# A chunked linear-attention layer and its squared-ReLU MLP on one core: first chunk loaded as pairs of tokens, second weight matrix on SyncE's queue

## The chip, the cores and the metric

The kernel runs on one core of a Trainium2 chip. A core has a matrix engine (TensorE, PE in the profile; its weight loads are PEld), a vector engine (VectorE, DVE), a scalar engine (ScalarE, ACT), GpSimd (POOL) and SyncE (SP), which here only issues transfers. SBUF is the on-chip memory with 128 partitions; PSUM holds what TensorE writes, in eight banks of 128 x 512 fp32. Sixteen DMA engines move data between HBM and SBUF. The metric is the device time of one execution in microseconds (us), the median of several runs.

## The reference

Two stages: an attention with a decaying state, then a feed-forward with squared ReLU. With B = 4 batches, H = 8 heads, S = 768 tokens, D = 48:

```python
for t in range(S):
    cur = np.einsum('bhd,bhe->bhde', u[None] * kt, vt)
    y[:, :, t] = np.einsum('bhd,bhde->bhe', rt, state + cur)
    state = w[None, :, :, None] * state + np.einsum('bhd,bhe->bhde', kt, vt)
x = y.transpose(0, 2, 1, 3).reshape(3072, 384)
h = np.maximum(x @ w_in, 0.0)          # w_in  384 x 2048
out = (h * h) @ w_out                  # w_out 2048 x 384
```

## The kernel before

The sequence is cut into six chunks of L = 128 tokens. A unit is one batch's chunk; unit i is batch i mod 4 of chunk i div 4, so there are 24, and units 0 to 3 are the first chunk, with no state yet. Inside a chunk the recurrence becomes products of matrices: r and k are scaled by powers of w (rows count up for r, down for k), a masked 128 x 128 product of them per head weighs v, the state of the chunk before adds its part, and the diagonal term with u is done elementwise.

The order of all work is written out by hand as a string, ORDER: 966 steps, each with a name, its indices, the engine (A ScalarE, D VectorE, G GpSimd, P TensorE, S SyncE) and the buffers it takes. Each engine gets its own steps in this order and works through them in order. The names:

- ld.x.i loads r, k or v of unit i: 128 tokens on 128 partitions, 8 pieces of 48 floats (192 bytes) for each. w and u load the decay and bonus rows; shw and shu spread them over the partitions (wb, ub); logw, Wk, Wt, WkS, WtS make the powers of w; wc, WLcol, WLm the power for a whole chunk.
- kh.i and rh.i multiply k and r by those powers into rk (bf16); T.i transposes rk on TensorE (eight transposes into one bank) and Tc.i copies it to rkT. From unit 7 on XB.i does this by a transposing transfer.
- A.i: eight products (four pairs of heads by two heads) of rkT into two banks; Bm.i.h masks them. Y.i: Bm by v (vb, bf16), plus rkT by the state S0W from chunk 1 on. U.i: k by v, for the state; S0, ts and S update it.
- P0, P1, du, dv: the diagonal term; xs.i adds it to Y. X.i and xTc.i (or the transfer xX.i) transpose x into xT.
- F1.g.s: x by W1 for group g of units, 512 columns of one bank; re and sq are ReLU and square. F2.i.q: four products of unit i with quarter q of W2, added up in one bank; os.i copies the sum, out.i stores it. F2c splits the last unit by columns.
- lW.0.s loads slice s of W1 in fp32 to a staging buffer wsa, cW.0.s casts it to bf16. W.0.2 (a slice of W1) and W.1.0 to W.1.3 (W2) are transfers on GpSimd's queue that cast on the way.
- Z.n.b is filler: n products of identity by identity (in fours, as one product of 512 columns) into bank b.

GROUPS lists how many units share one F1: units 0 and 1 are groups of one (products of 128 columns), all others pairs (256 columns). PSUM is split: four banks for attention ("bank"), two for F1 ("bH"), two for F2 ("bO"); the powers of w for the first chunk live in the last two ("early").

Of the kernel before, what the change touches and what calls it, by code (L numbers as in the profile page):

```python
# [28 lines left out]
Y.2:P/1 xs.2:D/2 re.1.3:A/0 X.0:P/3 F1.1.0:P/0 xTc.0:A/1 F1.0.0:P/1 dv.3:G Y.3:P/2 xs.3:D/3 X.2:P/1 ld.r.4:S/4 U.0:P/3
re.1.0:A/1 xTc.2:A/0 W.1.0:G F1.0.3:P/0 cW.0.5:G W.1.1:G X.3:P/2 cW.0.4:A xTc.3:A sq.1.0:A0/0 re.0.0:D/2 ld.k.4:S/4  # L30
ld.r.5:S/5 U.3:P/1 F1.0.2:P/1 WLcol:A re.0.3:D/3 ld.k.5:S/5 re.0.2:D/4 F1.1.2:P/0 sq.0.0:A0/1 W.1.2:G W.1.3:G ld.k.7:S/6
re.1.2:D/5 F1.2.1:P/1 ld.v.5:S/4 WkS:A F1.2.4:P/0 cW.0.3:G re.2.1:A/1 F1.2.5:P/1 re.2.4:D/2 U.1:P/2 F1.2.7:P/0
sq.0.2:A0/2 re.2.5:A/4 sq.1.3:D2/3 re.2.7:A/0 sq.2.1:D2/4 sq.2.4:D2/5 F1.0.1:P/1 F1.1.1:P/0 sq.0.3:D2/6 re.0.1:A/1
F1.2.3:P/1 re.1.1:A/2 sq.1.1:A0/7 sq.1.2:D2/8 WLm:G F2.0.0:P/1 S0.0:D re.2.3:D/3 F1.2.2:P/0 F2.1.0:P/0 F1.2.6:P/1 S0.3:D
re.2.2:A/2 F1.2.0:P/0 P0.4:G/4 sq.0.1:D2/9 kh.7:G/4 ld.v.4:S/5 F2.1.1:P S0.1:D ld.r.7:S/6 rh.4:D/5 sq.2.7:A0/10 kh.4:D
sq.2.5:A0/11 F2.0.1:P T.4:P/3 S0.2:D sq.2.3:A0/12 P0.5:G/0 sq.2.2:A0/13 rh.5:D/6 F2.0.2:P P1.4:D re.2.0:A/5 Tc.4:A/4
kh.5:D F2.1.2:P ld.r.6:S/2 ld.k.6:S/0 sq.2.0:D1/14 P1.5:G A.4:P/1/2 T.5:P/0 Tc.5:A/5 du.4:D/4 F2.0.3:P Bm.4.0:D/2
ld.v.7:S/6 F2.1.3:P os.0:D/0 os.1:A/1 A.5:P/3/0 Bm.4.1:D/0 vb.4:A/4 vb.5:A/5 F2.3.0:P/1 re.2.6:A/1 F2.2.0:P/0 Bm.5.0:D/4
ld.r.9:S/0 F2.2.1:P Y.4:P/1 du.5:D/0 Bm.5.1:D/5 U.5:P/2 Y.5:P/3 vb.7:A/6 dv.4:G F2.2.2:P sq.2.6:D1/15 ld.k.9:S/1
xs.4:D/4 dv.5:G rh.7:G F2.3.1:P X.4:P/0 kh.6:G/3 xs.5:D/0 X.5:P/1 ld.v.6:S/0 ts.5:D/0 P0.7:D/1 xTc.5:A/1 rh.6:D F2.3.2:P  # L40
xTc.4:A P1.7:D XB.7:S/6 F2.2.3:P kh.9:D/2 P0.9:D/3 T.6:P/3 rh.9:D F1.3.4:P/0 ld.k.10:S/2 F2.3.3:P Tc.6:A/0 P0.6:D/2
ld.k.8:S/3 vb.6:A/7 re.3.4:A/0 F1.3.3:P/1 A.6:P/2/1 re.3.3:A/4 ld.r.8:S/1 P1.6:G ld.v.8:S/1 os.3:D/2 A.7:P/0/3
F1.3.1:P/0 du.7:D/1 F1.3.5:P/1 S.5:G Bm.6.0:D/3 kh.8:G/1 U.7:P/2 Bm.6.1:D/1 ld.v.10:S/2 re.3.1:A/3 du.6:D/2 re.3.5:A/2
dv.6:G Bm.7.1:D/2 U.4:P/1 Bm.7.0:D/0 sq.3.3:A0/16 F1.3.0:P/0 F1.3.2:P/1 re.3.0:A/5 sq.3.1:A0/17 Y.6:P/3 dv.7:G Y.7:P/0
ld.v.9:S/3 F1.3.7:P/0 ts.4:D/1 XB.9:S/1 out.3:S re.3.2:A/1 xs.6:D/1 sq.3.0:A0/18 vb.8:A/2 U.6:P/1 os.2:D/3 rh.8:G
kh.10:G/0 X.6:P/3 XB.8:S/3 sq.3.2:A0/19 ld.k.11:S/4 F1.3.6:P/1 F2.5.0:P/1 ld.r.10:S/3 F2.4.0:P/0 xs.7:D/2 X.7:P/0
F2.4.1:P xTc.6:A/2 ld.r.11:S/4 F2.5.1:P ts.7:D/0 re.3.6:A/4 re.3.7:D/3 xTc.7:A F1.4.4:P/1 P0.8:G/4 kh.11:G/6 F1.4.6:P/0
S.4:D ld.r.12:S/5 ld.k.13:S/5 sq.3.7:A0/20 ts.6:D/1 P1.8:D sq.3.4:A0/21 du.8:D/3 ld.r.13:S/6 sq.3.5:A0/22 S.7:D
# [69 lines left out]
def kernel(  # L118
# [66 lines left out]
    def bank(var, kind="b"):  # L185
        return banks[first[kind] + slot[var]]
# [65 lines left out]
    def loaded(x, i):  # L252
        return ld[x][slot[f"{x}{i}"]]
# [308 lines left out]
```

## Time and profile before

| | us |
|---|---|
| median of 3 runs | 174.04 (173.41 to 174.83) |
| profiled execution, span | 172.5 |
| TensorE busy | 161.6 |
| VectorE busy | 130.3 |
| ScalarE busy | 111.1 |
| GpSimd busy | 80.8 |
| of TensorE: F1 products (line 445) | 74.9 |
| F2 products (line 472) | 69.3 |
| filler (line 498) | 9.5 |

Times in the profile count from the first instruction of the span. A busy matrix engine is not one at its peak: products are pipelined, and a product's listed duration is its passage, not its distance to the next. In rows of the timeline the columns are start, duration (of the first to the last of a run of equal instructions), engine, line, operation, what is written and read, count, and in brackets the idle time before and what ended it. In rows of the groups come the count, the busy time and the mean in ns, then the idle time before them. In rows of the windows come, for each engine, busy time and instructions, then the granted clock, the busy share of the DMA engines and GB/s.

### The profile page before, as it was taken

The numbers are of one execution on the slowest core, as the hardware profiler recorded it, in microseconds if no ns is written. First come the engines' busy times: TensorE is split into PE (matmuls) and PEld (weight loads), VectorE is DVE, ScalarE is ACT, GpSimd is POOL, SyncE is SP. The second block draws the span as 40 slices with busy tenths as digits, with TensorE's granted clock in tenths as the row PEclk, the third lists the DMA queues.
The fourth block names the chain that finished last, engine by engine and source line by source line (L and its number), as shares of the span: only waits on it lengthen the run. The fifth ranks groups of instructions, "written<-read, shape, count | busy, mean of one in ns | idle before, by whom it ended". The sixth has DMA issues, their size and how long they took to land.

```text
span 172.5 us, 4388 instructions
## 1 busy us (share of the span) xinstructions
PE 161.6 (94%) x1702; PEld 121.2 (70%) x1702; DVE 130.3 (76%) x259; ACT 111.1 (64%) x207; POOL 80.8 (47%) x98
## 2 busy tenths in 40 slices
PE   3976799979999999999999999999999999999992
PEld 1444788745788787787778768777778778777671
DVE  5768977739999896598789889888889894538300
ACT  2358787746379899858649647848858726532430
POOL 5644895108659298966937364047660204000000
PEclk9999999999999999999999999999999999999999
DMA  5999899989999989979999997998988330331022
GB/s 99 223 244 306 227 188 207 195 166 200 204 212 184 202 177 214 241 174 184 204 189 215 177 229 153 180 181 186 154 217 159 85 114 4 87 141 48 23 78 84
DMA packets 105588, 29.13 MB, mean 169 GB/s; under 512 B 98008, under 2 KB 105568, under 8 KB 105568
## 3 DMA queue, kind: packets, MB, share of 16 engines
q1 hardware_dynamic: 103672, 26.95, 72.7%
q0 software_dynamic: 1744, 1.77, 6.1%
q8 instruction: 13, 0.21, 0.5%
q10 hardware_dynamic: 152, 0.14, 0.2%
q14 instruction: 7, 0.06, 0.1%
HBM read 20.46 MB, written 4.72 MB: 146 GB/s over the span
## 4 chain that ended last, share of the span: by engine, by line
PE 76%; DMA 12%; SPq 8%; ACT 1%; POOL 1%; issue 1%; DVE 0%; POOLq 0%
PE bank L472 33%; PE bank L445 31%; DMA ldk<-in_k_dram 8%; SPq L320 6%; DMA wsa<-in_moe_w_in_dram 4%; PE bank L376 3%; PE bank L394 2%; PE bank L392 2%; SPq L324 2%; PE bank L403 2%; PE bank L486 2%; PE bank L429 1%; PE bank L363 1%; ACT W L260 1%; POOL urow L218 0%
## 5 line engine op out<-in xcount | busy, mean ns | idle before, releaser
L445 PE MATMUL bank<-xT,W 128*128 128x256 bf16 (+1 forms) x624 | 74.9, 264 | 0.2
L472 PE MATMUL bank<-W,hq 128*128 128x384 bf16 x368 | 69.3, 326 | 0.0
L453 ACT ACTIVATE hr<-bank 128x512 bf16<-128x512 f32 x75 | 44.4, 596 | 32.6 <-PE bank L445 27.1
L445 PEld LDWEIGHTS <-W 128*128 128x128 bf16 x624 | 55.2, 98 | 10.6 <-DVE hr L455 0.3
L472 PEld LDWEIGHTS <-hq 128*128 128x128 bf16 x368 | 34.8, 98 | 17.6
L460 ACT ACTIVATE hq<-hr 128x512 bf16<-128x512 bf16 x65 | 39.1, 628 | 0.3
L384 DVE TENSOR_TENSOR Bm<-bank,maskJT 128x512 bf16<-128x512 f32 x48 | 31.3, 684 | 7.3 <-PE bank L376 7.2
L346 POOL TENSOR_TENSOR P<-P,ub 128x384 f32<-128x384 f32 x15 | 16.1, 1079 | 13.9 <-DVE P L342 13.6
L455 DVE TENSOR_SCALAR hr<-bank 128x512 bf16<-128x512 f32 x21 | 14.3, 687 | 8.5 <-ACT hq L460 3.8
L342 POOL TENSOR_TENSOR P<-ldr,ldk 128x384 f32<-128x384 f32 x14 | 14.3, 1022 | 9.6 <-DMA ldk<-in_k_dram 6.0
L336 POOL TENSOR_TENSOR rk<-ldk,Wkhat 128x384 bf16<-128x384 f32 x10 | 10.0, 996 | 16.9 <-DMA ldk<-in_k_dram 16.9
L411 DVE TENSOR_TENSOR xs<-bank,dv 128x384 bf16<-128x384 f32 x24 | 13.0, 552 | 5.0 <-POOL dv L354 2.8
L354 POOL TENSOR_TENSOR dv<-ldv,du 128x384 f32<-128x384 f32 x18 | 14.8, 829 | 0.0
L349 DVE TENSOR_REDUCE du<-P 128x8 f32<-128x384 f32 x24 | 13.0, 544 | 0.6 <-POOL P L346 0.4
L260 ACT COPY rkT<-bank 128x1024 bf16<-128x1024 bf16 x7 | 7.1, 1012 | 9.1 <-PE bank L363 9.1
L339 POOL TENSOR_TENSOR rk<-ldr,Wt 128x384 bf16<-128x384 f32 x9 | 9.0, 996 | 7.0 <-DMA ldr<-in_r_dram 7.0
L260 ACT CAST vb<-ldv 128x384 bf16<-128x384 f32 x19 | 9.6, 511 | 4.1 <-DMA ldv<-in_v_dram 4.1
L498 PE MATMUL bank<-identity 128*128 128x512 bf16 x29 | 9.5, 471 | 2.7 <-POOL identity masks.py:199 2.7
L260 ACT COPY os<-bank 128x384 f32<-128x384 f32 (+1 forms) x15 | 7.0, 469 | 6.8 <-PE bank L472 4.5
L262 DVE COPY os<-bank 128x384 f32<-128x384 f32 (+1 forms) x10 | 5.2, 524 | 7.9 <-PE bank L486 4.3
L394 PE MATMUL bank<-vb,Bm 128*128 128x48 bf16 x192 | 11.0, 183 | 0.0
L464 DVE TENSOR_TENSOR hq<-hr 128x512 bf16<-128x512 bf16 x27 | 10.9, 432 | 0.0
(66 smaller groups left out, 166.5 us busy)
## 6 DMA issues: line engine op xcount, KB each, us to landing
ldk<-in_k_dram SPq DMA_DIRECT2D x24, 192.0 KB, 3.6
ldr<-in_r_dram SPq DMA_DIRECT2D x24, 192.0 KB, 3.6
ldv<-in_v_dram SPq DMA_DIRECT2D x24, 192.0 KB, 4.0
out_dram<-os SPq DMA_DIRECT2D x23, 192.0 KB, 2.3
wsa<-in_moe_w_in_dram SPq DMA_DIRECT2D x7, 384.0 KB, 5.6
W<-in_moe_w_out_dram POOLq DMA_DIRECT2D x4, 384.0 KB, 9.9
rkT<-rk SPq DMA_TRANSPOSE x17, 3.5
W<-in_moe_w_in_dram POOLq DMA_DIRECT2D x1, 192.0 KB, 6.3
```

The lines of the kernel that those rows point to most:

```text
L260: e.copy(o, a)
L342: e.tensor_mul(P0b[slot[f"P{i}"]], loaded("r", i), loaded("k", i))
L346: e.tensor_mul(t, t, ub)
L349: e.tensor_reduce(dub[slot[f"dv{i}"]], P0b[slot[f"P{i}"]], axis=mybir.AxisListType.X, op=ALU.add)
L354: e.tensor_mul(dvb[slot[f"dv{i}"]], loaded("v", i), t)
L384: e.tensor_mul(Bmb[slot[f"Bm{i}{h}"]], heads(bank(f"bA{i}{h}"), 128), mask_b)
L394: e.matmul(y[:, hc, D * h : D * (h + 1)], m[h][:, hc, :], vb[:, 2 * hc + h, :], start=(c == 0), stop=True, skip_group_check=True,)
L445: e.matmul(hp[:, fi, :], W1[f // 2][:, c, 128 * (f % 2) : 128 * (f % 2 + 1)], xt[:, c, :], start=(c == 0), stop=(c == CCH - 1), skip_group ...
L453: e.activation(hr, hp, AF.Relu)
L455: e.tensor_scalar_max(hr, hp, 0.0)
L460: e.activation(hq, hr, AF.Square)
L472: e.matmul(bank(f"bO{i}", "bO")[:, 0:d_model], hqb[slot[f"hq{g},{f // m}"]][:, at : at + L], W2[q][:, f % 4, :], start=(f == 0), stop=(f = ...
```

## The change

- **The first chunk in pairs.** Batches 0 and 1, and batches 2 and 3, are loaded together: batch 2p to partitions 0 to 63 and batch 2p + 1 to partitions 64 to 127, two neighbouring tokens on one partition. A piece is then 384 bytes; there are 12 such transfers (ldp) in place of 12 ld. Unit 2p + j now means the tokens of parity j of both batches. Two sets of powers of w are made (Wkp, Wtp), one for each parity, from column exponents that GpSimd writes.
- **Products on quarters.** Rows 0 to 63 and 64 to 127 belong to different batches, so A of units 0 to 3 is done for each half of rows apart (16 products, 64 output partitions each), Y sums over both parities (32 products of 64 rows, 64 output partitions and 48 columns), and U runs once for a pair (16 products of 64 rows) and gives both batches' state. T and Tc of these units are done apart for r and k, four transposes into half a bank.
- **W2 by SyncE.** The DMA casts on GpSimd's queue are gone. W2 comes in eight slices in fp32 (lW.1.s), each partition reading two whole rows (3,072 bytes) and W1 in eight (lW.0.s), through nine shared staging buffers st (also those of the pairs); cW casts them, on ScalarE six times, GpSimd nine times, VectorE once.
- **w** is spread by one transfer to all 128 partitions on SyncE's queue, without wrow and shw.
- **GROUPS** is twelve pairs; the eight PSUM banks are one pool; F2 may take W2's parts in any order (F2.i.f0.nf starts at product f0), and `summed` tells which product is the first and the last of a bank.
- **ORDER** is new throughout (976 steps).

The start of the new order:

```
tab:A nat:G ldp.r.0.1:S/0 w:S logw:A Wtp.0:A ldp.r.0.0:S/0 rh.0:D/0 Z.60.7:P T.r.0:P/0 Wtp.1:A rh.1:D/0 T.r.1:P/0
ldp.k.0.1:S/1 Wkp.1:A ldp.k.0.0:S/1 kh.1:G/1 Wkp.0:A kh.0:D/1 Tc.r.1:A/0 u:S shu:D ldp.k.1.0:S/2 Tc.r.0:A/0 Z.10.7:P
T.k.1:P/1 Tc.k.1:A/1 Z.16.7:P A.1:P/2/3 P0.1:D/0 P0.0:G/1 P1.1:D du.1:D/0 ldp.k.1.1:S/2 kh.2:D/2 T.k.0:P/1 kh.3:G/2
ldp.r.1.0:S/3 T.k.3:P/4 ldp.r.1.1:S/3 rh.2:G/3 P0.3:D/2 wc:S Bm.1.1:D/0 WkS:A Tc.k.0:A/1 Z.8.0:P A.0:P/5/6 Bm.0.1:D/1
Bm.0.0:D/2 Bm.1.0:D/3 T.r.2:P/7 rh.3:G/3 Z.7.0:P T.r.3:P/7 P1.0:G ldp.v.0.1:S/4 ldp.v.0.0:S/4 dv.1:G vb.1:A/0 du.0:D/1
T.k.2:P/4 dv.0:D vb.0:A/1 U.p0:P/0/1 Z.13.6:P Y.0:P/3 ld.r.4:S/0 xs.0:D/0 Tc.r.2:A/2 Y.1:P/6 xs.1:D/1 Tc.r.3:A/2 Tc.k.2:A/3
A.2:P/5/7 Bm.2.1:D/4 P1.3:G du.3:D/2 WtS:A ld.k.4:S/0 WLcol:A WLm:G S0.0:D lW.0.5:S/5 cW.0.5:G Tc.k.3:A/3 kh.4:G/4 lW.0.2:S/6
cW.0.2:A A.3:P/2/4 Bm.3.0:D/5 X.0:P/3 xTc.0:A/0 ldp.v.1.0:S/7 X.1:P/6 xTc.1:A/0 ld.k.5:S/1 kh.5:D/5 ldp.v.1.1:S/7 vb.2:A/2
rh.4:G/4 F1.0.2:P/7 re.0.2:A/0 F1.0.5:P/3 re.0.5:A/1 T.4:P/0 Bm.2.0:D/0 ld.r.5:S/1 rh.5:D/5 lW.0.6:S/8 cW.0.6:A vb.3:G/3
U.p1:P/6/2 P0.2:G/3 dv.3:G Bm.3.1:D/1 T.5:P/5 Tc.4:A/4 lW.0.1:S/0 cW.0.1:G P1.2:D Y.2:P/7 F1.0.6:P/3 re.0.6:A/2 S0.2:D
...
```

Its last three steps on TensorE are F2.22.4.4, F2c.23.0 (256 columns) and F2c.23.1 (128 columns); before, the last unit, 22, had its 128 columns first and its 256 columns last.

The core of the rest:

```diff
-GROUPS = [1, 1, 2, 2, 2, 2, 2, 2, 2, 2, 2, 2, 2]
+GROUPS = [2, 2, 2, 2, 2, 2, 2, 2, 2, 2, 2, 2]
+    stb = bufs("st", [128, CCH * 256], FP32)
...
+    def two(x, b):
+        t = src[x]
+        return bass.AP(
+            tensor=t.tensor, offset=t.offset + b * H * S * D,
+            ap=[[2 * D, L // 2], [S * D, H], [1, 2 * D]],
+        )
...
+        def ldp(e, x, p, b):
+            e.dma_start(out=staged(f"{x}P{p}").rearrange("p (h x) -> p h x", h=H)[rows[b]], in_=two(x, 2 * p + b))
...
         def lW(e, a, s):
+            t = staged(f"ws{a}{s}")
+            if a == 0:
+                e.dma_start(out=t.rearrange("p (c n) -> p c n", c=CCH), in_=w_in_t[:, :, 256 * s : 256 * (s + 1)])
+            else:
+                e.dma_start(out=t, in_=w_out_p[s])
...
-        def W(e, a, s):
-            e.dma_start(out=rows2(W2[s], s) if a else W1[s], in_=weights(a, s))
...
         def A(e, i):
+            if i < B:
+                tk, tr = [rkTb[slot[f"rkT{x}P{i // 2}"]].rearrange("q (j c) t -> q j c t", j=2) for x in "kr"]
+                for hc in range(HP):
+                    for h in range(2):
+                        q = slice(64 * h, 64 * h + D)
+                        for p in rows:
+                            e.matmul(
+                                heads(bank(f"bA{i}{h}"), 128)[p, hc, :].rearrange("p (j t) -> p j t", j=2),
+                                tk[q, i % 2, hc, p],
+                                tr[q, :, hc, p],
+                                start=True, stop=True, skip_group_check=True,
+                            )
+                return
...
         def Y(e, i):
+            if i < B:
+                both = [i - i % 2, i - i % 2 + 1]
+                at = slice(64 * (i % 2), 64 * (i % 2) + 64)
+                for hc in range(HP):
+                    for h in range(2):
+                        for z in both:
+                            for p in rows:
+                                e.matmul(
+                                    y[p, hc, D * h : D * (h + 1)],
+                                    Bmb[slot[f"Bm{z}{h}"]][p, hc, at],
+                                    vbb[slot[f"vb{z}"]][p, 2 * hc + h, :],
+                                    start=(z == both[0]), stop=(z == both[1]), skip_group_check=True,
+                                )
+                return
...
         def U(e, i):
+            if isinstance(i, str):
+                n = int(i[1:])
+                for hc in range(HP):
+                    for j in range(2):
+                        for b, p in enumerate(rows):
+                            e.matmul(
+                                heads(bank(f"bU{2 * n + b}"), 2 * D)[:, hc, :],
+                                pair(rk[slot[f"rkkP{n}"]][p], j, hc),
+                                vbb[slot[f"vb{2 * n + j}"]][p, 2 * hc : 2 * hc + 2, :].rearrange("p a b -> p (a b)"),
+                                start=(j == 0), stop=(j == 1), skip_group_check=True,
+                            )
+                return
...
-        def F2(e, i, q):
+        def F2(e, i, f0, nf):
...
-            for f in range(4 * q, 4 * q + 4):
+            for f in range(f0, f0 + nf):
                 at = L * n * (f % m) + L * j
+                summed[i] += 1
...
-                    start=(f == 0), stop=(f == FCH - 1), skip_group_check=True,
+                    start=(summed[i] == 1), stop=(summed[i] == FCH), skip_group_check=True,
```

More of the change, by code (lines that the diff above doesn't have):

```diff
@@ L32 @@
[L32 to L36, printed above, removed]
```

365 lines of the change are left out of this document (203 added, 162 removed).

## The prediction

> **What bounds the kernel now.** I read the page's head first, then the windows, the chain, and the timeline of the first 40 us, to see which engine is full and from when.
>
> ```profile
> span 172.5 us, 4388 instructions
> PE 161.6 (94%) x1702; PEld 121.2 (70%) x1702; DVE 130.3 (76%) x259; ACT 111.1 (64%) x207; POOL 80.8 (47%) x98
> PEclk9999999999999999999999999999999999999999
> ```
> ```profile
> 0.00:10.00 10.00, 7.30 (x37) 3.40 (x38) 7.11 (x25) 3.91 (x5) 5.95 (x16) 1.00 0.85 170
> 10.00:20.00 10.00, 6.96 (x110) 4.93 (x107) 7.65 (x15) 7.05 (x11) 5.12 (x7) 1.00 0.98 263
> 20.00:40.00 20.00, 18.07 (x218) 14.53 (x215) 13.71 (x28) 13.70 (x27) 9.46 (x14) 1.00 1.06 196
> 40.00:169.33 129.33, 129.32 (x1349) 98.32 (x1347) 101.79 (x194) 86.09 (x166) 60.23 (x64) 1.00 0.75 160
> ```
>
> From 40 us to the last product TensorE has no gap (129.32 of 129.33 us, clock 1.00). That stage costs its products and nothing else, so a change can win only by entering it with less work left, or at the tail. Up to 40 us TensorE is short of inputs: it idles and runs filler (the Z steps), while the DMA share is near 1.
>
> ```profile
> 1.16 0.70 POOL urow L218
> 24.58 13.90 DMA ldk<-in_k_dram
> 39.12 0.62 PE bank L363 x8
> 39.74 1.30 PE bank L472 x8
> 49.68 0.55 PE bank L376 x16
> 51.99 1.31 PE bank L445 x12
> 151.04 1.95 PE bank L472 x12
> 166.68 2.65 PE bank L486 x32
> ```
>
> The chain enters through one load: k of unit 5, issued at 24.58, takes 13.90 us, in the time in which the W2 transfers of GpSimd's queue are under way. TensorE's products end at 166.68 + 2.65 = 169.33; the tail to the span's end is 172.5 − 169.33 = 3.17 us. The span lies 174.04 − 172.5 = 1.54 us under the median of the runs; I add that back at the end.
>
> Prices, from the chain above: an F1 step of six products is half of 1.31 = 0.655 us; four F2 products are a third of 1.95 = 0.65. The others:
>
> ```profile
> 2.70 5.18 PE L498 MATMUL bank<-identity 128*128 128x512 bf16 x13 [2.70 <-POOL identity masks.py:199]
> 9.69 0.49 PEld L363 LDWEIGHTS <-rk 128*128 128x128 bf16 x8
> 15.09 1.24 PE L498 MATMUL bank<-identity 128*128 128x512 bf16 x5
> 16.23 0.30 PEld L394 LDWEIGHTS <-Bm 128*128 128x128 bf16 x8
> 17.36 0.17 PEld L429 LDWEIGHTS <-xs 128*128 128x128 bf16 x3 [0.34 <-DVE xs L411]
> 19.11 0.83 PE L445 MATMUL bank<-xT,W 128*128 128x128 bf16 x12
> ```
> ```profile
> L453 ACT ACTIVATE hr<-bank 128x512 bf16<-128x512 f32 x75 | 44.4, 596 | 32.6 <-PE bank L445 27.1 <-DVE Bm L384 3.8 <-ACT os L260 0.7
> L460 ACT ACTIVATE hq<-hr 128x512 bf16<-128x512 bf16 x65 | 39.1, 628 | 0.3
> L384 DVE TENSOR_TENSOR Bm<-bank,maskJT 128x512 bf16<-128x512 f32 x48 | 31.3, 684 | 7.3 <-PE bank L376 7.2
> L260 ACT CAST vb<-ldv 128x384 bf16<-128x384 f32 x19 | 9.6, 511 | 4.1 <-DMA ldv<-in_v_dram 4.1
> L260 ACT COPY rkT<-bank 128x1024 bf16<-128x1024 bf16 x7 | 7.1, 1012 | 9.1 <-PE bank L363 9.1
> L260 ACT COPY xT<-bank 128x384 bf16<-128x384 bf16 x14 | 6.6, 480 | 1.8 <-PE bank L429 1.7
> L339 POOL TENSOR_TENSOR rk<-ldr,Wt 128x384 bf16<-128x384 f32 x9 | 9.0, 996 | 7.0 <-DMA ldr<-in_r_dram 7.0
> L376 PEld LDWEIGHTS <-rkT 48*128 48x128 bf16 x192 | 5.5, 94 | 4.7 <-issue 2.5 <-ACT rkT L260 2.2
> L260 ACT CAST W<-wsa 128x768 bf16<-128x768 f32 x4 | 3.6, 890 | 0.8 <-DMA wsa<-in_moe_w_in_dram 0.8
> L486 PE MATMUL bank<-W,hq 128*128 128x256 bf16 x16 | 1.9, 272 | 0.0
> L262 DVE COPY os<-bank 128x128 f32<-128x128 f32 x1 | 0.3, 291 | 4.3 <-PE bank L486 4.3
> ```
>
> **The change, part by part.** I walk TensorE's new order in three legs: to its first F1 step, from there to F2.0.12.4 (the step that needs the last slice of W2), and from there to the end.
>
> *Work left after F2.0.12.4.* Before, from F2.0.3 on (the chain's piece at 39.74), 169.33 − 39.74 = 129.6 us of work are left, without a gap: 80 F1 steps, 86 F2 steps, and A, Y, U, X of the later units. Counting the new order behind F2.0.12.4's start: 76 F1, 82 F2, one A, two Y and two X fewer, the 16 U the same. An A is eight products of 0.55/16 = 0.034, so 0.28; a later Y is twelve of 0.30/8 = 0.0375, so 0.45; an X three of 0.055. Less: 4 × 0.655 + 4 × 0.65 + 0.28 + 0.9 + 0.33 = 6.7. So 129.6 − 6.7 = 122.9 us are left.
>
> *The quarter tiles.* A of the first four units becomes 16 products instead of 8, Y 32 instead of 8, U 16 per pair instead of 8. No row shows a product on a quarter. Nearest is A on halves: 0.034 us apart. Floor: all four quarters at once, 0.017. Ceiling: a weight load fully exposed, 0.094. I take 0.034, since A's halves already overlap their loads: A 0.55, Y 1.1, U 0.55. All of it lies on TensorE's path, 4 × 16 + 4 × 32 = 192 products of A and Y.
>
> The Trainium skill, TensorEngine Tiling (Array Packing), Key Properties and Restrictions, speaks against the change: column tiling switches the fast weight load off, and a change of tiling mode drains the array. By TensorE: Matmul & The Clock Gate, LDWEIGHTS, a load then costs its columns over 1.2 GHz, an estimated 53 ns for 64, which would put the sum 192 × 0.019 = 3.6 us higher. No row here shows it; as a mechanism of this kernel it is the first rival.
>
> *First leg.* GpSimd no longer fills wrow and fills urow (0.7 us) only later, so identity comes at about 2.70 − 0.70 = 2.0. Z.60 is 15 products of 512: 13 took 5.18, two more 0.25 each (1.24/5): to 7.6. Its transposes (four of 0.055 each for r0, r1) follow. Then ScalarE paces: three copies of half an rkT (0.6 each by 596 ns for 512 columns; a whole one 1.01) end at 10.0, A.1 to 10.6; T.k.0, its copy behind WkS (0.6) to 11.55; Z.8, which writes the same bank and so waits, to 12.0; A.0 to 12.55. Three maskings at 0.684 on VectorE give 14.7; TensorE fills that with six transposes, U, Z (3 more) to 14.85. Y.0 and Y.1 to 17.05, A.2, A.3 to 18.15, X to 18.5, two xT copies (0.48) to 19.4: F1 starts at **19.4**, on 256 columns. Before it started at 19.11, on 128. ScalarE has the cast of W1 slice 2 (0.89) done by 17.3.
>
> Do loads come in time? Rates by the windows:
>
> ```profile
> 8.00:10.00 2.00, 2.00 (x22) 1.36 (x21) 1.95 (x5) 1.01 (x1) 1.33 (x2) 1.00 1.15 225
> 12.00:14.00 2.00, 1.49 (x16) 0.84 (x12) 2.00 (x4) 0.47 (x1) 1.04 (x2) 1.00 1.01 295
> 14.00:16.00 2.00, 1.37 (x13) 0.90 (x14) 2.00 (x5) 2.00 (x4) 0.98 (x1) 1.00 1.03 288
> 16.00:18.00 2.00, 1.58 (x31) 1.17 (x30) 1.48 (x4) 2.00 (x4) 0.00 (x0) 1.00 1.14 323
> ```
> ```profile
> DMA to landing us min/median/max: 2.8/3.6/3.7
> ```
>
> Loads of r, k, v alone (192-byte pieces, the first window) run at 225 GB/s: 196.6 KB in 0.87 us. With W1 (1-KB pieces) it is 302 on average: 393 KB in 1.30. A paired load has 384-byte pieces: between 0.87 and 0.61 (323 GB/s); I take 0.75. The first lands at 0.8 + 2.8 = 3.6, so the stream starts at 2.85. Up to W1 slice 2: ten paired, w (0.65), two r/k, two slices: 2.85 + 7.5 + 0.65 + 1.74 + 2.6 = 15.3, in time. Up to the last W2 slice: 12 × 0.75 + 0.65 + 12 × 0.87 + 16 × 1.30 = 40.9: lands at 43.7, cast by 44.6. SyncE's queue has the W2 slices between loads of units 4 to 9; the latest of those that this stretch needs, r6, stands four slices ahead of the end: 43.7 − 5.2 = 38.5, for T.6 near 42. W2's casts were free before (done in the transfer); now eight of 0.89 lie on ScalarE (four), GpSimd (three), VectorE (one). A new wait: on GpSimd WLm stands behind ScalarE's WLcol (16.2) and ahead of the cast of W1 slice 5 and of kh.4, rh.4; with 0.8 + 0.9 + 2 × 1.0 that is 19.9, and T.4, who waits for it, comes at 20.7.
>
> *Second leg.* 20 F1 (13.1), 10 F2 (6.5), T.4 to T.6 (eight of 0.055: 1.3), U (0.55), Y.2, Y.3 (2.2), Y.4, Y.5 (0.9), A.4, A.5 (0.55), X (0.65): 25.75. From 19.4 that is 45.15. ScalarE beside it: 12 re (7.2), 10 sq (6.3), five casts (4.5), two rkT (2.0), three vb (1.55), three xT (1.45) = 23.0, hence 42.4 without waits; in its order it waits for F1 and X steps some 2.5 us and for the transposes 0.9, so its cast of the last slice ends at 45.85. That is 0.7 behind TensorE: F2.0.12.4 at **45.85**.
>
> *Third leg.* 45.85 + 122.9 = 168.75, against 169.33. What goes is the wait for k of unit 5; what takes its place is ScalarE's queue.
>
> *Tail.* Before, the last half is 256 columns (ScalarE copy, then its own issue); now 128, with a 0.29-us copy and the other half away already. I take 0.25 off: 2.9.
>
> Sum: 168.75 + 2.9 + 1.54 = **173.2 us**, 0.5% under 174.04.
>
> **The rivals.** *Quarter tiles at full price.* If loads of half the columns are exposed (half of 0.094 = 0.047), 192 × 0.013 = +2.5: **175.7**; at 0.06 it is +5, 178.2. It decides from 0.047 on, in A and Y of units 0 to 3. For it: no row shows quarters overlapping. Against: A's loads mostly overlap. By the Trainium skill's 53 ns, above, it would be 176.8.
>
> *Loads late.* All now stands in one queue. Should a W slice take 1.45, the last lands at 46.1, cast at 47.0: +1.15, **174.4**; at the 225 GB/s of small pieces, 1.75, it is +6. For it: 20 to 40 us ran at 196 GB/s with the share at 1.06. Against: the W2 transfers count there by what they write, 384 KB of bf16 for 768 KB read (row below), so more was moved than the figure says.
>
> ```profile
> W<-in_moe_w_out_dram POOLq DMA_DIRECT2D x4, 384.0 KB, 9.9
> ```
>
> *Faster.* Four quarters at once (0.017) brings the first F1 to the ScalarE bound, about 18.2, and Y.2, Y.3 off 1.1; with W slices at 323 GB/s and ScalarE's waits shrunk by another 1.0 the last cast ends at 43.7: 43.7 + 122.9 = 166.6, **171.0**. For it: VectorE and ScalarE were 70% busy there. Against: three things must go right together.
>
> *The change doesn't do what it says* (384-byte pieces no faster): 12 × 0.12 = 1.4 us later, the last cast at 46.0 instead of 44.6, still no later than ScalarE reaches it: 173.2 to 173.5.
>
> **How the numbers follow.** About 1% (1.7 us) is what a measurement of this kernel tells from no change. Forecast and hidden variants (172.3 to 175.7): 0.42. Faster rival: 0.33, above what its conditions alone give, since my legs take each disputed price in the middle and the order can hide more than I let it. Quarter tiles 0.14, loads 0.07, and 0.04 for new waits after 46 us (VectorE is 79% busy there): slower 0.25. The range leaves out a tenth each side: 170.8 to 177.0; the likeliest case's own is 172.3 to 175.0.
>
> **What would show it.** Right: first F1 near 19.4, F2.0.12.4 near 45.9 right after ScalarE's cast, no TensorE gap after it, A on quarters at 0.55 per unit, no load over 8 us. Wrong: pitch of A or Y over 0.047; W2 slices landing after 46; TensorE idle after 50; a clock row under 9 (not expected: Z has 27 wide products for 29).

## The result, and the profile after

The changed kernel takes 198.08 us (median of 4, 197.55 to 200.67) where the kernel before, run beside it, takes 174.44: a ratio of 1.135, 95% interval 1.128 to 1.141. Ratios and intervals, here and below, leave out runs over 1.5% above the fastest of the same kernel. The forecast was 173.2, the range 170.8 to 177.0. The profiled execution has a span of 195.8 us, against 172.5.

The head of the page of the changed kernel:

```profile
span 195.8 us, 4600 instructions
PE 172.1 (88%) x1795; PEld 123.9 (63%) x1795; DVE 147.9 (76%) x262; ACT 104.9 (54%) x192; POOL 105.8 (54%) x125
PEclk9999799999999996985999999999999999999999
DMA  4999999999898694599899957799389024021133
```

TensorE is no longer busy without a gap, its clock row has dips, and the DMA row falls to 6, 4 and 5 in three slices between 64 and 83 us. The same row of the kernel before has no digit under 7 from the second slice to the thirtieth:

```profile
DMA  5999899989999989979999997998988330331022
```

The windows of the changed kernel (length, then busy time of PE, PEld, DVE, ACT and POOL, clock, DMA share, GB/s) put most of the loss between 60 and 120 us:

```profile
60.00:70.00 10.00, 8.89 (x96) 6.94 (x94) 9.37 (x16) 7.60 (x14) 9.86 (x11) 1.00 0.89 150
70.00:80.00 10.00, 6.54 (x54) 4.57 (x55) 4.38 (x9) 1.55 (x3) 6.33 (x7) 0.83 0.64 134
80.00:90.00 10.00, 5.13 (x47) 3.50 (x46) 7.09 (x12) 4.69 (x8) 2.59 (x3) 0.84 0.83 135
100.00:120.00 20.00, 18.37 (x215) 13.45 (x214) 19.52 (x33) 9.48 (x20) 16.95 (x18) 1.00 0.90 193
```

Between 70 and 80 us every engine is idle much of the time, and the DMA engines with them: not one full engine, but a chain. TensorE's waits behind 46 us in the changed kernel (total, times, longest) and the longest pieces of the chain there name it:

```profile
PE bank L433 <- DMA rkT<-rk: 9.5, 4, 4.3
PE bank L531 <- DMA xT<-xs: 1.4, 2, 0.7
```
```profile
65.04 8.37 DMA rkT<-rk
73.45 0.61 PE bank L433 x8
74.06 1.39 PE bank L559 x4
...
85.93 3.39 DMA rkT<-rk
89.37 0.61 PE bank L433 x8
89.98 3.84 PE bank L559 x12
```

A step of A waits for its transposing transfer, which takes 8.37 us from issue to landing (the median before was 3.5), and behind each gap the products run at half clock for a while (the granted clock is 0.50 from 87 to 93 us): twelve F2 products take 3.84 us, where the chain before had 1.95.

The steps that the prediction named, from TensorE's timeline and the end of the chain of the changed kernel:

```profile
13.29 0.42 PE L422 MATMUL bank<-rkT,rkT 48*64 48x128 bf16 x16
17.33 1.13 PE L457 MATMUL bank<-vb,Bm 64*64 64x48 bf16 x60
21.24 2.12 PE L531 MATMUL bank<-xT,W 128*128 128x256 bf16 x12 [1.53 <-ACT xT L262]
49.40 2.76 PE L559 MATMUL bank<-W,hq 128*128 128x384 bf16 x16
```
```profile
190.45 2.65 PE bank L573 x32
```

F1 starts at 21.24. The 16 products at 49.40 are F2.0.8.4, F2.2.8.4, F2.0.12.4 and F2.1.12.4, so F2.0.12.4 starts two steps of 0.65 later, at 50.70. The last product ends at 190.45 + 2.65 = 193.10. The same points read in four later kernels (named below):

| | F1 | F2.0.12.4 | last product ends | third leg |
|---|---|---|---|---|
| forecast | 19.4 | 45.85 | 168.75 | 122.9 |
| changed kernel | 21.24 | 50.70 | 193.10 | 142.4 |
| outputs in halves | 21.23 | 51.33 | 184.94 | 133.6 |
| the same, whole loads | 19.68 | 49.20 | 182.97 | 133.8 |
| new start, old rest, outputs in halves | 21.12 | 50.98 | 176.85 | 125.9 |

The forecast span of 171.65 is missed by 24.15 us: first leg 1.84, second 3.01, third 19.5, tail −0.2.

### The profile page after: what moved, and what is told of

Read it like the earlier page. It is cut to its first block, busy times and chain, and to the rows that moved or that the text cites. A ratio compares the mean times of both kernels' runs of the same rounds, so it can differ in the third digit from the quotient of the medians.

```text
span 195.8 us, 4600 instructions
## 1 busy us (share of the span) xinstructions
PE 172.1 (88%) x1795; PEld 123.9 (63%) x1795; DVE 147.9 (76%) x262; ACT 104.9 (54%) x192; POOL 105.8 (54%) x125
## 4 chain that ended last, share of the span: by engine, by line
PE 42%; DMA 17%; DVE 15%; SPq 12%; POOL 6%; issue 5%; ACT 1%; DVEq 0%; POOLq 0%
PE bank L559 20%; PE bank L531 16%; DMA rkT<-rk 6%; SPq L344 6%; DVE Bm L446 4%; DMA xT<-xs 4%; SPq L347 3%; DMA st<-in_moe_w_in_dram 3%; DVE hq L550 2%; DMA ldv<-in_v_dram 2%; DMA st<-in_moe_w_out_dram 2%; PE bank L433 2%; DVE xs L497 1%; SPq L352 1%; DVE ts L507 1%
## 5 line engine op out<-in xcount | busy, mean ns | idle before, releaser
L531 PE MATMUL bank<-xT,W 128*128 128x256 bf16 x576 | 70.9, 274 | 3.1 <-ACT xT L262 1.5
L539 ACT ACTIVATE hr<-bank 128x512 bf16<-128x512 f32 x67 | 38.9, 593 | 47.0 <-PE bank L531 45.7
L541 DVE TENSOR_SCALAR hr<-bank 128x512 bf16<-128x512 f32 x29 | 19.7, 683 | 16.2 <-ACT hq L546 8.0
L550 DVE TENSOR_TENSOR hq<-hr 128x512 bf16<-128x512 bf16 x37 | 24.7, 682 | 5.2 <-ACT hr L539 4.8
L446 DVE TENSOR_TENSOR Bm<-bank,maskJT 128x512 bf16<-128x512 f32 x40 | 26.0, 678 | 3.1 <-PE bank L433 3.1
L433 PE MATMUL bank<-rkT 48*128 48x128 bf16 x160 | 7.9, 231 | 9.6 <-DMA rkT<-rk 9.5
L433 PEld LDWEIGHTS <-rkT 48*128 48x128 bf16 x160 | 4.9, 99 | 13.1 <-DMA rkT<-rk 10.7
L510 POOL TENSOR_TENSOR S0W<-ts,WLm 128x384 bf16<-128x384 f32 x10 | 10.1, 1014 | 5.6 <-DVE ts L507 5.6
L507 DVE TENSOR_TENSOR ts<-bank,S0W 128x384 f32<-128x384 f32 x16 | 8.7, 547 | 5.7 <-PE bank L489 5.5
L262 ACT COPY xT<-bank 128x384 bf16<-128x384 bf16 x12 | 5.6, 477 | 11.1 <-PE bank L515 11.1
```

Source lines behind the costliest of these rows:

```text
L433: e.matmul(heads(bank(f"bA{i}{h}"), 128)[:, hc, :], t[p0 : p0 + D, HP + hc, :], t[p0 : p0 + D, hc, :], start=True, stop=True, skip_group_c ...
L446: e.tensor_mul(o, a, mask_b)
L531: e.matmul(hp[:, fi, :], W1[f // 2][:, c, 128 * (f % 2) : 128 * (f % 2 + 1)], xt[:, c, :], start=(c == 0), stop=(c == CCH - 1), skip_group ...
L539: e.activation(hr, hp, AF.Relu)
L541: e.tensor_scalar_max(hr, hp, 0.0)
L550: e.tensor_mul(hq, hr, hr)
```

## The experiments

Times are in us, with the kernel before run beside them. That one's median moved from 173.1 to 177.0 between the groups of runs, so kernels of different groups are compared by their ratios (95% interval in brackets).

| kernel | time | before | ratio |
|---|---|---|---|
| h1, new start, old rest | 189.76 | 175.36 | none |
| h2, old start, new rest | 191.47 | 175.36 | 1.095 [1.088, 1.102] |
| k3, new order, old engines | 225.37 | 175.36 | 1.284 [1.272, 1.297] |
| e1, outputs in halves | 190.99 | 176.19 | 1.084 [1.074, 1.094] |
| h1s, h1 with outputs in halves | 181.69 | 176.19 | 1.033 [1.023, 1.043] |
| before, outputs two by 64 | 186.74 | 176.19 | 1.057 [1.045, 1.070] |
| e2, e1 with W2 by GpSimd | 191.90 | 177.04 | 1.087 [1.078, 1.097] |
| e4, h1s with W2 by GpSimd | 183.49 | 177.04 | 1.040 [1.032, 1.049] |
| e5, e1 with whole loads | 187.43 | 177.04 | 1.060 [1.051, 1.068] |
| e3b, e1, two copies for a square | 195.62 | 177.04 | 1.105 [1.094, 1.115] |
| k4, h1s with the new engines | 192.82 | 176.13 | 1.098 [1.091, 1.105] |
| k3s, k3 with outputs in halves | 215.73 | 176.13 | 1.229 [1.221, 1.237] |
| e3c, e1, one copy for a square | 190.32 | 176.13 | 1.082 [1.076, 1.087] |
| e3d, e1, short squares | 188.92 | 173.09 | 1.092 [1.087, 1.096] |
| e6, e1, GpSimd's steps short | 187.17 | 173.09 | 1.078 [1.070, 1.085] |
| e8, e1, both short | 187.33 | 173.09 | 1.080 [1.073, 1.087] |

h1 has no ratio, since only one of its times is left for it: they are 186.65 and three from 189.63 to 189.97.

### Which part of the order: h1, h2, k3

```diff
 ORDER (h1): the new steps through Tc.6:A/6, then all other steps as the old ORDER has them
 ORDER (h2): the old steps through Tc.6:A/0, then all other steps as the new ORDER has them
 ORDER (k3): the new one, each elementwise step behind Tc.6 on the engine that it had before
```

> The changed kernel's first 275 steps (through the copy of unit 6's transposes), then the 701 steps that remain in the order of before, on its engines. Theory 'rest' (the new order behind 46 us makes the idle time): the start still reaches F2.0.12.4 at about 50.7 us, TensorE then has 122.9 us of work without a gap worth naming, ends near 174 and the time is 177 to 179 us. Rival 'start' (what the start leaves behind, late loads and late slices of W2, makes the gaps whatever order follows): 190 us or more, with TensorE idle between 70 and 90 us as in the changed kernel.

> The mirror image: before's start through the copy of unit 6's transposes, then the changed kernel's remaining steps in their order and on their engines. Theory 'rest': the same 19 us of idle time and half clock come back behind a good start, 188 to 194 us, with transposing transfers of 6 to 8 us ahead of A of unit 10. Rival 'start': 174 to 177 us.

> The changed kernel with its order kept, but each elementwise step behind the copy of unit 6's transposes on the engine that it had before (ScalarE 154 instead of 133 of them, VectorE 90 instead of 95, GpSimd 54 instead of 70). Theory 'engines' (more work on GpSimd, and VectorE slowed beside it, makes rk and so the transposing transfers late): VectorE's squares of hr fall from about 0.85 us towards 0.43 between 100 and 150 us, most of the 13 us of idle time goes, 180 to 186 us. Rival 'queue' (the place of the transposing transfers behind loads in SyncE's queue makes them late, whichever engine makes rk): 193 to 198 us, and A of unit 10 still waits for 3 us or more.

Both halves lose: h1 is 11 to 15 us slower than before, h2 16. Neither theory had that. h2's time lies in the range of theory 'rest', but not by its mechanism: TensorE's waits behind 46 us there are for results of VectorE, some 9 us, and 1.4 for transposing transfers. k3, meant to relieve GpSimd, lost 15 points more. What helped was a pattern in SyncE's timeline. In the changed kernel (start, time of the issue, line):

```profile
63.35 0.63 SPq L603 DMA_DIRECT2D out_dram<-os  x1
64.03 0.91 SPq L344 DMA_DIRECT2D ldk<-in_k_dram  x1
65.04 4.91 SPq L413 DMA_TRANSPOSE rkT<-rk  x1
...
71.31 0.57 SPq L603 DMA_DIRECT2D out_dram<-os  x1
...
73.79 4.46 SPq L344 DMA_DIRECT2D ldr<-in_r_dram  x1
78.36 0.68 SPq L603 DMA_DIRECT2D out_dram<-os  x1
...
79.86 5.34 SPq L413 DMA_TRANSPOSE rkT<-rk  x1
```

Each of these stalls comes two or three issues behind an output, and the three outputs are out.2, out.3 and out.1; behind out.0, at 132.05, the next issue takes 3.29. Behind outputs of later units none takes 3 (one more, 4.49 at 44.04, comes ahead of all outputs, behind slices of W2). The first four units' outputs are the ones whose access the change altered, to two times 64 rows. During the stalls the 16 DMA engines are nearly idle (windows of the changed kernel):

```profile
67.00:68.00 1.00, 1.00 (x9) 0.61 (x8) 1.00 (x2) 0.97 (x3) 1.00 (x2) 1.00 0.16 43
77.00:78.00 1.00, 1.00 (x14) 0.73 (x12) 0.53 (x2) 0.48 (x1) 1.00 (x2) 1.00 0.13 48
```

A share of 0.13 is two engines of 16.

### The outputs of the first chunk: e1, h1s, before with the cost added, outputs alone

```diff
 def out(e, i, half=None):          # e1, h1s
-        o = AP(offset=..., ap=[[S * d_model, 2], [2 * d_model, L // 2], [1, d_model]])
+        for b in range(2):
+            o = AP(offset=... + b * S * d_model, ap=[[2 * d_model, L // 2], [1, d_model]])
+            e.dma_start(out=o, in_=osb[slot[f"os{i}"]][rows[b], c])
 def out(e, i, half=None):          # before, outputs two by 64
+    if i < B:
+        o = AP(offset=..., ap=[[d_model, 2], [2 * d_model, L // 2], [1, d_model]])
```

> The changed kernel with one edit: the output of each of the first four units (two times 64 rows, every other row of two batches) goes out as two transfers of 64 partitions instead of one. In the changed kernel these four outputs are issued at 63.35, 71.31, 78.36 and 132.05 us, and behind each SyncE's queue stalls: issues of 4.91, 4.46, 5.34 and 3.29 us, in which the DMA share falls to 0.13 to 0.18, about two of 16 engines. Theory 'output' (the transfer of two times 64 rows runs on two DMA engines, and what is queued behind it waits): no issue over 3 us behind 60 us, the transposing transfer for A of unit 10 lands within 5 us of its issue, the 9.5 us in which TensorE waits for rkT go, and with them most of the half clock: 181 to 186 us. Rival 'shared' (the idle time comes from GpSimd and VectorE, which make rk late): 194 to 199 us. Rival 'halves no better' (64 rows with a gap are slow in any form): the same stalls, 196 to 200 us.

> The same edit in the kernel of the new start and the old rest (189.76 us). Its stalls stand behind the same four outputs too (issue of 3.83 us at 59.04 behind 58.28; of 4.56 at 85.06 behind 77.53 and 78.88; 3.24 at 113.6 behind 109.89). Theory 'output': the idle time behind 46 us (about 9 us) falls to 3 or less, 178 to 182 us. Rivals: 187 to 191 us.

> The kernel before with the suspected cost added and nothing else: the output of its first four units is written as two times 64 rows with every other row (within the same 128 rows, so these rows come out in another order). Theory 'output': each of the four transfers keeps two DMA engines busy for 4 to 5 us, transposing transfers behind them take 6 to 8 us to land and TensorE, without a gap now behind 40 us, gets gaps; the outputs come at places where the queue has more slack than in the changed kernel, so 177 to 188 us. Rivals: 174 to 175.5 us, no issue over 3.2 us behind 40 us.

> Not the reference's computation: outputs alone, each waited for, then four in a row, then one ahead of a transposing transfer and three loads; in three forms: 128 rows side by side, two times 64 every other row in one transfer, and the same in two transfers. Theory 'output': the middle form takes 5 us or more where the others take about 2, its DMA share is 0.12 to 0.15, four in a row take 16 to 20 us against 3 to 5, and the transposing transfer behind it lands 3 to 5 us later than behind the others. Rival (the stalls have nothing to do with the outputs): all three forms within 0.5 us of each other. Rival 'rows': the middle form and its halves are both slow.

The kernel of outputs alone, on VectorE's timeline (in brackets the wait for the transfer): 128 rows side by side, two times 64 in one transfer, the same in two transfers; then the transposing transfer behind each of the three, issued at 74.77, 81.89 and 92.99:

```profile
14.48 0.06 DVE L620 MEMSET os<- 128x1 f32 x1 [2.04 <-DMA out_dram<-os]
...
23.30 0.06 DVE L620 MEMSET os<- 128x1 f32 x1 [6.69 <-DMA out_dram<-os]
...
39.52 0.06 DVE L620 MEMSET os<- 128x1 f32 x1 [2.95 <-DMA out_dram<-os]
...
77.92 0.15 DVE L672 CAST sink<-rkT 128x1 f32<-128x1 bf16 x1 [3.60 <-DMA rkT<-rk]
...
88.81 0.15 DVE L672 CAST sink<-rkT 128x1 f32<-128x1 bf16 x1 [7.59 <-DMA rkT<-rk]
...
96.29 0.15 DVE L672 CAST sink<-rkT 128x1 f32<-128x1 bf16 x1 [4.53 <-DMA rkT<-rk]
```

2.04, 6.69 and 2.95 us; the transposing transfer takes 3.15, 6.92 and 3.30 from its issue. Four of the middle form in a row take 18.5 us. While the middle form runs alone, the DMA share is 0.13 (kernel of outputs alone, windows; VectorE and GpSimd are the only engines with columns; in the first row transfers of the plain form run):

```profile
12.00:16.00 4.00, 0.50 (x4) 0.00 (x0) 1.00 0.26 98
18.00:22.00 4.00, 0.00 (x0) 0.00 (x0) 1.00 0.13 38
```

The Trainium skill, DMA: Bandwidth & Descriptors, section "Rules for kernel authors", states it: the outermost dimension sets the number of engines, one of size c under 16 confines the transfer to at most c. With an outermost 2 that is the 0.13 measured here; the halves have 64 outermost.

In the kernels the theory holds too: e1 gains 5 points (the third leg 8.8 us), h1s gains 3 on h1's fastest run (186.65/175.36 = 1.064) and 5 on its median (1.082), and the kernel before, given nothing but the two-times-64 outputs, loses 5.7% and shows waits for rkT of 6.3 us, where TensorE did not wait at all. In e1 no issue behind 60 us takes over 2.5 us, and TensorE's wait for rkT falls from 9.5 to:

```profile
PE bank L433 <- DMA rkT<-rk: 2.3, 3, 1.9
```

But e1 is at 190.99, not at the 181 to 186 expected: a second cause remains. h1s, expected at 178 to 182, fits; so what remains of e1's loss beyond h1s, 5 points, lies in the new remaining order, in its places or its engines.

### The start: prices alone, whole loads, W2 back on GpSimd's queue

> Not the reference's computation: only transfers in groups, each group begun when the one ahead has landed, and then VectorE's squares, maskings and casts alone, beside GpSimd's scaling products, beside its W casts and beside its memsets. By the prediction a paired load (384-byte pieces, half of the partitions) takes 0.75 us, 0.61 to 0.87, in a stream; a single load 0.87; a slice of W1 or W2 1.30. Theory 'loads' (paired loads use the DMA engines worse because each fills half of the partitions): 0.95 to 1.1 us each, and the same bytes on all 128 partitions cheaper per byte. Theory 'shared' (VectorE slows beside GpSimd): squares go from 0.42 to 0.8 or more beside the scaling products; rival: they stay at 0.42 to 0.5 and the slow squares in the changed kernel have another cause.

In this kernel a copy reads each load when it has landed (VectorE's timeline): two paired loads apart, then one whole transfer of the same bytes apart:

```profile
18.26 0.15 DVE L622 COPY sink<-st 128x1 f32<-128x1 f32 x1 [1.78 <-DMA st<-in_k_dram]
...
20.22 0.15 DVE L622 COPY sink<-st 128x1 f32<-128x1 f32 x1 [1.80 <-DMA st<-in_v_dram]
...
29.00 0.15 DVE L622 COPY sink<-st 128x1 f32<-128x1 f32 x1 [1.35 <-DMA st<-in_k_dram]
...
30.50 0.15 DVE L622 COPY sink<-st 128x1 f32<-128x1 f32 x1 [1.35 <-DMA st<-in_v_dram]
```

1.96 us for two paired loads, so 0.98 each, and 1.50 for the same bytes on 128 partitions (0.75 a load). A single load of 192-byte pieces came at 0.91 to 0.94, most slices of W1 at 1.13, most of W2 at 0.98. The issue of two paired loads takes SyncE 1.31 us, so the issues do not set the 1.96. The forecast had 0.75 for a paired load and 1.30 for a slice.

```diff
 def ldp(e, x, p, b):               # e5: one for each pair p
-    two(x, 2 * p + b) -> rows[b]
+    AP(offset=... + 2 * p * H * S * D, ap=[[2 * D, L], [S * D, H], [1, 2 * D]]) -> 128 partitions
 ORDER (e2, e4):
-lW.1.0 ... lW.1.7 and cW.1.0 ... cW.1.7
+W.1.1:G behind cW.0.1, W.1.0:G behind cW.0.0, W.1.2:G behind cW.0.7, W.1.3:G behind kh.7
```

> The changed kernel with the outputs in halves, and each two paired loads (64 partitions each) replaced by one transfer of the same bytes to 128 partitions; it reads 256 tokens of one batch in place of 128 of two, so the first chunk is computed on other tokens. In the transfers measured alone two paired loads take 1.96 us and one whole one 1.50. Theory 'loads' (the half-filled loads pace the start): six times 0.46, so F1 starts 1.5 to 2.5 us earlier than 21.2 and F2.0.12.4 2 to 3 us earlier than 51.3; 187.5 to 189 us. Rival: the casts and the order pace the start, F1 within 0.7 us of 21.2, 190 to 192 us.

> The changed kernel with the outputs in halves (190.99 us), and W2 back on GpSimd's queue in four transfers that cast on the way, so that the eight casts of W2 slices on ScalarE, GpSimd and VectorE go. Theory 'casts' (the on-chip casts hold up the engines ahead of F2.0.12.4, which starts near 51.3 us): F2.0.12.4 comes 2 us or more earlier, 187 to 189 us. Rival 'transfers' (the 16 DMA engines are full until 47 us in any case, share 1.0 between 28 and 48 us, and a second queue only shares them): F2.0.12.4 within 1 us of 51.3, 190 to 193 us.

> The same W2 edit in the kernel of the new start and the old rest with the outputs in halves (181.69 us). Theory 'casts': 178 to 180 us. Rival 'transfers': 181 to 184 us.

Whole loads bring F1 to 19.68 and F2.0.12.4 to 49.20, 1.55 and 2.1 us earlier, and the end with it (span 185.8 against 187.9 us; the ratio falls by 2.4 points): the paired loads pace the start. Taking the casts off the chip's engines gains nothing in either kernel (1.087 against 1.084, 1.040 against 1.033), and in e2 F2.0.12.4 starts at 52.43, so rival 'transfers' is the nearer one.

### The remaining order: engines, work or places

In the kernel of prices VectorE made six squares of hr and six maskings alone, then beside eight of GpSimd's products, started together:

```profile
109.14 3.68 DVE L706 TENSOR_TENSOR Bm<-bank,maskJT 128x512 bf16<-128x512 f32 x6
...
114.70 8.73 POOL L729 TENSOR_TENSOR rk<-P,wb 128x384 bf16<-128x384 f32 x8
...
114.84 6.79 DVE L702 TENSOR_TENSOR hq<-hr 128x512 bf16<-128x512 bf16 x6
121.55 3.67 DVE L706 TENSOR_TENSOR Bm<-bank,maskJT 128x512 bf16<-128x512 f32 x6
```

A square takes 1.13 us there (6.79/6), the pitch of GpSimd's products (8.73/8 = 1.09), where five alone took 1.76, 0.35 each; the maskings, which read PSUM, do not change (3.67 against 3.68; the first three still ran beside the products, which end at 123.43). Squares and products take turns. The Trainium skill, SBUF — State Buffer, section "Who interferes with whom", has it as an exclusive lock on ports that the two engines share: a VectorE instruction with two inputs in SBUF contends with a GpSimd instruction that reads SBUF; the trace agrees (1.13 against 0.35 us). Does that make the remaining 5 points?

```diff
 def sq(e, g, s, form):             # g >= 2, on VectorE
-    e.tensor_mul(hq, hr, hr)
+    for _ in range(2): e.tensor_copy(hq, hr)                      # e3b; once in e3c
+    e.tensor_mul(hq[:, 0:64], hr[:, 0:64], hr[:, 0:64])           # e3d, e8
 kh, rh, P0, P1, dv, vb, S on GpSimd behind Tc.6                   # e6, e8: in 67 of 70 steps
-    e.tensor_mul(o, a, b)
+    e.tensor_mul(o[:, 0:1, :], a[:, 0:1, :], b[:, 0:1, :])
 ORDER (k4): h1s, each elementwise step behind Tc.6 on the new engine
 ORDER (k3s): e1, each on the old engine
```

> The changed kernel with the outputs in halves, and VectorE's squares of hr from the third group of units on (32 of them) replaced by two copies of hr each, which have one input in place of two; the squaring is left out there. Order, buffers and waits stay. Alone a square takes 0.35 us, beside GpSimd's products 1.13, a copy is not slowed. Theory 'shared' (behind 52 us VectorE, slowed beside GpSimd, is what TensorE waits for: squares 0.66 us on average there, against 0.44 before): VectorE's busy time falls by 8 us or more, GpSimd's products shorten a little, most of the 5 us of TensorE's waits for VectorE's results and transposing transfers go: 184 to 187 us. Rival 'order' (the waits come from where steps stand, not from slow squares): 189 to 192 us.

> The kernel of the new start and the old rest with outputs in halves (1.033 of before), and each of its remaining elementwise steps on the engine that the changed kernel gives it (128 of 407 steps change engine; GpSimd 70 instead of 54). Theory 'engines' (more work on GpSimd and on VectorE beside it is what costs): 1.07 to 1.10 of before, VectorE's squares at 0.6 us or more on average behind 52 us. Theory 'order': 1.03 to 1.05. Rival 'fit' (order and engines were made for each other, and either alone costs more than both): 1.12 or more.

> The changed kernel with outputs in halves (1.084 of before) and each remaining elementwise step on the engine that it had before. Theory 'engines': 1.03 to 1.05. Theory 'order': 1.08 to 1.10. Rival 'fit': 1.12 or more; with the outputs in one piece this kernel took 1.284, 15 points more than the changed kernel.

> The changed kernel with outputs in halves, and each of VectorE's 32 squares from the third group of units on replaced by one copy of hr (0.29 us alone against 0.41); the squaring is left out there. If TensorE waits for VectorE behind 52 us, as with two copies (VectorE 9.3 us busier, some 4 us longer), VectorE gets 5 us or more less busy there and the time falls by 2 to 3 us, 1.065 to 1.075 of before. If VectorE is not what it waits for: 1.08 to 1.09.

> The changed kernel with outputs in halves, and VectorE's squares from the third group of units on made on 64 of 512 columns, in those buffers that were filled once before; the other columns keep what was there, so that part of the squaring is left out. Order, engines, buffers and waits stay. Theory 'work' (VectorE's and GpSimd's load between 60 and 120 us is what TensorE waits for): VectorE gets 8 us or more less busy behind 52 us and the time falls to 1.05 to 1.07 of before. Theory 'places' (steps stand where their inputs come late, whatever each costs): 1.075 to 1.09.

> The changed kernel with outputs in halves, and GpSimd's products and casts behind the copy of unit 6's transposes made on one head of eight (where the buffer was filled before); the other heads keep what was there. Theory 'work': VectorE's squares fall from 0.66 us on average to 0.45 or less although nothing on VectorE is changed, rk comes earlier, 1.03 to 1.06 of before. Theory 'places': 1.075 to 1.09.

> Both edits at once. Theory 'work': no less than the old remaining order reaches, 1.02 to 1.045 of before, with under 2 us in which TensorE is idle behind 60 us. Theory 'places': 1.06 to 1.085, and the same waits for transposing transfers as without the edits.

The crossed kernels do not separate order from engines. k4 (1.098) fits the theory 'engines', k3s (1.229) is far outside it and fits 'fit': presumably a step moved to another engine without a new place in the order holds up what stands behind it there. e3b lost 2 points with VectorE 7.9 us busier over the run, but e3c gained nothing. That a copy is not slowed was wrong: the casts alone in the kernel of prices ran when GpSimd's products had ended, and e3c's copies took 0.547 us on average, 0.28 at the least.

The last three settle what it is not. In e6 VectorE's squares behind 52 us fall to their time alone, 0.42 us each as listed, though nothing on VectorE was changed (first e1, then e6):

```profile
L550 DVE TENSOR_TENSOR hq<-hr 128x512 bf16<-128x512 bf16 x31 | 20.0, 661 | 5.2 <-ACT hr L539 4.8
```
```profile
L555 DVE TENSOR_TENSOR hq<-hr 128x512 bf16<-128x512 bf16 x32 | 13.1, 424 | 7.1 <-ACT hr L544 6.7
```

Yet the time hardly moves: e3d, e6 and e8 stand at 1.092, 1.078 and 1.080, each interval overlapping that of e1. The window from 60 to 120 us of e1, of e8 and of h1s, columns as above:

```profile
60.00:120.00 60.00, 54.87 (x564) 40.54 (x563) 57.16 (x94) 34.76 (x66) 47.69 (x49) 0.97 0.91 186
```
```profile
60.00:120.00 60.00, 53.76 (x586) 41.10 (x580) 47.13 (x95) 35.69 (x68) 15.36 (x49) 1.00 0.98 193
```
```profile
60.00:120.00 60.00, 59.20 (x636) 45.39 (x637) 50.15 (x97) 43.41 (x86) 34.20 (x36) 1.00 0.88 180
```

e8 takes 10 us off VectorE and 32 off GpSimd in that stretch, and TensorE is idle as long as in e1, some 5 to 6 us; h1s, with more on both engines than e8, has 0.8. So VectorE at 95% was not what bounds e1: with less work on it, other waits take the place of those for VectorE. What TensorE waits for in e8 behind 52 us:

```profile
PE bank L439 <- DMA rkT<-rk: 3.6, 4, 1.6
PE bank L537 <- DMA xT<-xs: 2.1, 1, 2.1
```

Transposing transfers, with the DMA share at 0.98. The share alone does not tell why: in the kernel before it is 0.93 between 60 and 120 us, and TensorE has no gap. Nor are the transfers slow: from issue to landing they take 3.7 us in the median in e8, 3.5 in the kernel before. They are issued late. GpSimd's last products for the rk of units 11 and 13 in e8, and SyncE's issues of their transfers:

```profile
68.51 0.29 POOL L373 TENSOR_TENSOR rk<-ldk,Wkhat 128x48 bf16<-128x48 f32 x1 [1.05 <-DMA ldk<-in_k_dram]
...
73.40 0.29 POOL L379 TENSOR_TENSOR rk<-ldr,Wt 128x48 bf16<-128x48 f32 x1
```
```profile
75.76 1.36 SPq L419 DMA_TRANSPOSE rkT<-rk  x1
...
77.86 1.36 SPq L419 DMA_TRANSPOSE rkT<-rk  x1
```

The rk are ready at 68.80 and 73.69; their transfers go out 7.0 and 4.2 us later, behind loads and outputs that SyncE issues without a pause, and land at 79.47 and 81.50, where two of the four waits for rkT end. Theory 'places' fits: the new order has these transfers too far back in SyncE's queue. An order with them moved was not tried, so what their places cost in all is argued, not shown. Nor is this all of it: in k4, as in h2, TensorE waits for results of VectorE, some 10 us.

No version beat the kernel before; the nearest, h1s, stands at 1.033.

## Why the prediction was wrong

- **The step that failed is the third leg**, "45.85 + 122.9 = 168.75": 122.9 us of TensorE's work is what is left, and it was taken to run without a gap because it did so before. It took 142.4: TensorE was idle for 13.3 us of it and busy for 129.1, part of that at half clock. Neither the prediction nor the list in "The change" has the new access of out for i < B. A transfer that stands in no sum at all, and that no compute waits for, held up the queue that the transposing transfers share. Undone, it gives 8.8 of the 19.5 us.
- Of the other 10.7, 7.7 go with the old remaining order behind the same start (133.6 to 125.9), and h2, with the outputs of before, shows that the new one costs behind the old start too (1.095). The prediction counted the new order's steps but not when their inputs come, and gave new waits behind 46 us a chance of 0.04; that case happened. Its sign of it, "TensorE idle after 50", was the right one to name, its reason (VectorE's load) is not borne out by e3d, e6 and e8. Of the last 3.0 us, between 125.9 and 122.9, TensorE is idle for 2.3; they were not traced further.
- **First leg**, 19.4 against 21.24: the term mis-sized is the paired load. "384-byte pieces: between 0.87 and 0.61" took the piece as what sets the price; at 0.98 measured, the ten up to W1's slice 2 cost 10 × 0.23 = 2.3 us more, and a kernel without that starts F1 at 19.68. The case "384-byte pieces no faster" was nearer, and dismissed as hidden.
- **Second leg**, 26.45 against 29.46 us: that ScalarE's casts of W2 pace it finds no support: without those casts it took 30.55 (e2, with the clock at 0.79 from 20 to 28 us) against 30.10 (e1). TensorE's work was sized right, 25.75 forecast and 25.96 busy in e1. What failed is that it was taken to wait 0.7 us in all: in e1 it is idle for 4.1, of which 1.4 for the second pair's v (vb) and 1.0 for unit 6's rk. In the changed kernel the first F1 comes behind a gap of 1.53 us, and the clock is at 0.50 from 22 to 25 us. Whole loads shorten the leg by 0.6 (30.10 to 29.52); what else makes the inputs late stays open. The slices of W2 themselves were cheaper than the 1.30 forecast.
- **Quarter tiles**: right that they cost little, and less than forecast. 16 products of A take 0.42 (0.55 forecast), 60 of Y 1.13, which is 0.019 each, near the floor of 0.017. The rival at 0.047, and the 53 ns estimated from the Trainium skill's TensorEngine Tiling (Array Packing) and TensorE: Matmul & The Clock Gate, are not what this trace shows.
- **Tail**: 2.9 forecast, 195.8 − 193.1 = 2.7.
- A clock row under 9 was "not expected" and came behind gaps of 1.5, 4.3 and 3.3 us. So the gaps cost more than their length.

## What to carry to other kernels

Read every access pattern that a diff changes, those of outputs too, and look at the size of its outermost dimension: a transfer on two DMA engines holds up whatever shares its queue. A stage without gaps says what its order was worth with its own timing; when order, engines or transfers change, its length is a floor and not a forecast. When TensorE idles between full engines, follow the wait to its releaser before blaming the fullest engine: taking 42 us of work away from VectorE and GpSimd bought nothing in e8.

## What the runs showed that was not expected

- The stall is visible in the issue, not only in the landing: a transposing transfer behind such an output takes 4.9 to 5.3 us to issue, against 1.2 to 1.6 in most issues before.
- Half of the partitions does not cost half: 0.98 us a load on 64 partitions, 1.50 for the double on 128.
- Behind TensorE's gap that ended at 87.18, its clock was at 0.50 until about 93.4, though TensorE was idle for only 1.6 us of that.
- Engines moved within an order written for others cost more than any single wait: 15 points in k3, as many in k3s.
